# A gated recurrence with a top-80 expert layer: full-width last loads, quarter-sized zero writes, unchained scatters and a shorter ranking

## The chip, the cores and the metric

One NeuronCore of a Trainium2 chip runs the whole program. The metric is the device time of one execution in microseconds (us); the runs shown are three executions of the kernel before. Matrix work runs on TensorE (PE; PEld are its weight loads), elementwise work on VectorE (DVE), ScalarE (ACT) and GpSimd (POOL), and transfers are issued by SyncE's queue (SP), a few by POOL and ACT. All transfers run on the same 16 DMA engines.

## The reference

The first half is a gated recurrence over 4 sequences of 5056 steps and 256 channels; the second half sends each of the 20224 results to one of 8 experts, keeps the 80 best per expert, and leaves every other row of the output zero.

```python
f = lower_bound + (1 - lower_bound) * sigmoid(f_logit)
for t in range(S):                       # S = 5056
    h = f[:, t] * h + (1 - f[:, t]) * x[:, t]
    y[:, t] = h
X = y.reshape(20224, 256)
logits = X @ w_gate                      # 8 experts
expert = argmax(logits); gate = softmax(logits)[expert]
out = zeros(20224, 256)
for e in range(8):
    tok = the 80 tokens of expert e with the largest gate
    out[tok] = gate[tok] * (relu(X[tok] @ w1[e]) @ w2[e])   # F = 1024
```

## The kernel before

**The stream.** Time is cut into 10 groups of 512 steps (the last has 448), and each group into 4 units, one for each sequence: 40 units. A unit `n` has one 512 KB load of `f_logit` and one of `x` (`load_f`, `load_x`, L235 and L241), issued three units ahead by SP; the last group loads 448 KB on 112 partitions. ACT makes the gate (`gate`, L249), POOL multiplies (`enter`, L253), PE transposes both into channels-by-time in PSUM (`to_channels`, L261, tiles `sp` and `up`), ACT turns `sp` into the decay in SBUF (`decay`, L271), and DVE runs the recurrence as two scans per unit (`scan`, L278). PE then makes the unit's gate logits (`logits`, L292). Once per group ACT copies the logits aside (`aside`), PE turns them by token (`by_token`, tile `lt`, L306), and DVE finds maxima and choices (`maxima` L318 and L319, `choice` L328 and L332). The PSUM pool of `up` has three buffers, two per unit; the turned candidates have a bank of their own (`ct`).

**The zeros.** The 20.7 MB of zeros of the output are written by SP from a zeroed DRAM tile, in 160 pieces of 128 KB (eighths of 20 strips, `clear_some`, L156): two behind each unit's loads for units 4 to 31, 16 behind the last load, 8 behind each of the first three weight keys, 16 more, and 4 behind each of the next 12 keys (`BESIDE`).

**The ranking.** When the last scan is done, POOL sums the exponentials of old groups (`halved`, L352) and makes their worths (`worth`, L366), PE turns them (`candidates`), DVE takes the top 8 of each of 8 parts (`peaks`, L383), `best` ranks those 64 into 12 (L386 to L389), which are put ahead of the two newest groups in `fresh`, and a second `best` ranks that. Selection, slots and token numbers follow up to L605.

**The experts.** Weights come in 16 keys of two 512 KB halves, through a ring of 6 halves (`weights`, L500 for w1 and L504 for w2), so key i waits until key i-3 has been used. The order is (1,0) (2,0) (1,1) (1,2) (2,1) (1,3) (2,2) (1,4) (2,3) (1,5) (2,4) (1,6) (2,5) (1,7) (2,6) (2,7), where (1,e) is w1 of expert e and (2,e) its w2. Expert e's 80 tokens are copied out of SBUF by DVE, ACT and POOL together (`gather`, L655, 24, 32 and 24 copies), scaled by DVE (L662), multiplied by w1 (`hidden`, L673) and w2 (`result`, L688), and scaled again (`finish`, L694); POOL sends them to their rows by one indirect DMA per expert (`scatter`, L697). A scatter may be sent only when all zeros have been issued, and waits for them to land. Each engine works its instructions in the order in which this loop writes them:

```python
for e in range(1, E):
    if e + 2 < E: gather(e + 2)
    if e + 1 < E:
        ps = hidden(e + 1); relu(e + 1, ps); more(1)   # one more key, and its zeros
    y_ps = result(e); more(1)
    if e + 2 < E: scaled(e + 2)
    finish(e, y_ps)
    scatters(e - 1)            # sends all that wait, if no zeros are left
```

Three keys are loaded before this loop's part of the code and three `more(1)` stand ahead of the loop.

Of the kernel before, what the change touches and what calls it, by code (L numbers as in the profile page):

```python
# [17 lines left out]
P = 128  # L18
TOP = 8
AWAY = 1.0e6  # L20
PAD = 104
# [6 lines left out]
def kernel(  # L28
# [25 lines left out]
    BESIDE = 4  # L54
# [5 lines left out]
    def first(g):  # L60
        return g * G
# [11 lines left out]
    assert B == R and C == R * R and all(size(g) % C == 0 for g in range(n_grp))  # L73
# [47 lines left out]
    NEW = DEEP + (n_grp - OLD) * P  # L121
# [3 lines left out]
    tops = consts.tile([P, NP, TOP], F32, name="tops")  # L125
    prev = consts.tile([P, 2 * TOP], F32, name="prev")
# [21 lines left out]
    ZQ = 8  # L148
# [4 lines left out]
    def clear(k, q=None):  # L153
        n = min(ZR, N // P - k) * D
        rows = slice(0, P) if q is None else ds(q * QP, QP)
# [28 lines left out]
    psu = psum.enter_context(tc.tile_pool(name="psu", bufs=3, space=PSUM))  # L184
    plg = psum.enter_context(tc.tile_pool(name="plg", bufs=1, space=PSUM))

    with tc.tile_pool(name="ld", bufs=4) as ld, \
# [47 lines left out]
        def load_f(n):  # L235
            g, b = divmod(n, B)
            fs[n] = ld.tile([P, R, D], F32, name="f_t", tag="f_t")
            nc.sync.dma_start(
                out=fs[n][:run(g)], in_=tiles(f_logit, b, g))

        def load_x(n):  # L241
            g, b = divmod(n, B)
            xs[n] = ld.tile([P, R, D], F32, name="x_t", tag="x_t")
            nc.sync.dma_start(
                out=xs[n][:run(g)], in_=tiles(x, b, g))

        def gate(n):
            s_t = sts[n] = fs.pop(n)[:run(n // B)]
            nc.scalar.activation(s_t, s_t, ACT.Sigmoid, scale=-1.0)  # L249

        def enter(n):
            u_t = uts[n] = xs.pop(n)[:run(n // B)]
            (nc.gpsimd if n else nc.vector).tensor_tensor(u_t, sts[n], u_t, ALU.mult)  # L253

        def to_channels(n, src, dst, pool, tag, in_time):
            k = run(n // B)
            for o in range(DC):
                ps = pool.tile([P, G], F32, name=tag, tag=tag)
                for r in range(R):
                    at = ps[:, r:R * k:R] if in_time else ps[:, ds(r * k, k)]  # L260
                    nc.tensor.transpose(at, src[n][:, r, ds(o * P, P)], ident[:k, :k])  # L261
                dst[n, o] = ps[:, :R * k]
            del src[n]
# [5 lines left out]
        def decay(n):  # L269
            for o in range(DC):  # L270
                nc.scalar.activation(columns(n, o).rearrange("c (p r) -> c p r", r=R),  # L271
                                     sps.pop((n, o)).rearrange("c (r p) -> c p r", r=R),
                                     ACT.Identity, scale=nomlb[:, ds(o, 1)], bias=1.0)

        def scan(n):
            for o in range(DC):
                h = columns(n, o)
                nc.vector.tensor_tensor_scan(  # L278
                    h, h, ups.pop((n, o)),
                    h_all[:, o, ds(spot(n) - 1, 1)] if n >= B else 0.0, ALU.mult, ALU.add)  # L280
# [60 lines left out]
        def sums(g0, g1):  # L341
            n = g1 - g0
            sms[g0] = gsm.tile([P, 1, C], F32, name="sm", tag="sm%d" % g0)
            nc.vector.tensor_reduce(
                sms[g0], exs.pop(g0).rearrange("p (g c e) -> p g c e", c=C, e=E), AX.X, ALU.add)
# [29 lines left out]
        def candidates(g0):  # L375
            ct = plg.tile([P, 2 * P], F32, name="ct", tag="ct")
            turned(g0, 2, ct)
            nc.scalar.copy(cand[:, ds(g0 * P, 2 * P)], ct)

        def peaks(g):  # L380
            for i, (g0, lo) in enumerate(parts):
                if g0 == g:
                    nc.vector.max(out=tops[:, i], in_=cand[:, lo:(g + 2) * P:2])  # L383

        def best(vals, src, rest):
            nc.vector.max(out=vals[:, :TOP], in_=src)  # L386
            nc.vector.match_replace(out=rest, in_to_replace=vals[:, :TOP], in_values=src,
                                    imm_value=GONE)
            nc.vector.max(out=vals[:, TOP:], in_=rest)  # L389
# [16 lines left out]
        done_f = []  # L406

        for n in range(-AHEAD, n_unit):
            m = n + AHEAD
            for k in (m, m + 1):  # L410
                if k < n_unit and k not in done_f and (k == m or m >= LAST - 2):
                    done_f.append(k)
                    load_f(k)
            unit(load_x, m)
            if n == -1:
                spread_zeros()
            if n == -AHEAD:
                setup()
            if n + 2 < LAST:
                unit(gate, n + 2)  # L420
            unit(enter, n + 2)
            if n + 1 < LAST:
                unit(lambda m: to_channels(m, sts, sps, pss, "sp", False), n + 1)
                unit(decay, n + 1)
            if n + 2 == LAST - 1:
                gate(LAST)
            if n + 2 == LAST:
                to_channels(LAST, sts, sps, pss, "sp", False)
                decay(LAST)
                aside(OLD)  # L430
                exponentials(0, OLD)
            unit(lambda m: to_channels(m, uts, ups, psu, "up", True), n + 1)
# [14 lines left out]
        for k in range(0, OLD, OLD // 2):  # L447
            halved(k, OLD // 2)
            for g in range(k, k + OLD // 2, 2):
                worth(g, k, 2, nc.gpsimd)  # L450
                candidates(g)
                if g == 0:
                    aside(n_grp - 1)
                elif g == 2:
                    by_token(n_grp - 1)
        g = n_grp - 1
        peaks(0)
        peaks(2)
        maxima(g)
        fresh = plg.tile([P, NEW], F32, name="fresh", tag="lg")  # L460
        busy(pss, 8, "sp")
        exponentials(g, g + 1, aside=True)
        choice(g, nc.vector)
        sums(OLD, OLD + 1)
        worth(OLD, OLD, 1, nc.gpsimd)
        turned(OLD, 1, fresh[:, ds(DEEP, P)])
        sums(g, g + 1)
        worth(g, g, 1, nc.vector)
        turned(g, 1, fresh[:, ds(DEEP + P, P)])
# [24 lines left out]
    def weights(which, e):  # L494
        halves = []
        for i in range(2):
            t = wring.tile([P, DC * FH], F32, name="w_sb", tag="w_sb")
            if which == 1:
                t = t.rearrange("p (o f) -> p o f", o=DC)
                nc.sync.dma_start(out=t, in_=w1[e][:, ds(i * FH, FH)].rearrange(  # L500
                    "(o p) f -> p o f", p=P))
            else:
                t = t.rearrange("p (c d) -> p c d", c=CH)
                nc.sync.dma_start(out=t, in_=w2[e][ds(i * FH, FH)].rearrange(  # L504
                    "(c p) d -> p c d", p=P))
            halves.append(t)
        return halves
# [27 lines left out]
    with tc.tile_pool(name="sel", bufs=1) as sel:  # L535
        vals2 = consts.tile([P, 2 * TOP], F32, name="vals2")
        rest = sel.tile([P, NEW], F32, name="rest")
        best(vals2, fresh, rest)
# [70 lines left out]
    def settle():  # L609
# [12 lines left out]
        nc.vector.tensor_reduce(d[:, 5:6], tops[:, :, TOP - 1], AX.X, ALU.max)  # L622
# [14 lines left out]
    def experts(again):  # L637
        with tc.tile_pool(name="xp", bufs=2) as xp, \
# [68 lines left out]
            waiting = []  # L707
# [135 lines left out]
```

## Time and profile before

| what | value |
|---|---|
| three executions | 260.38, 262.93, 266.25 us (median 262.93) |
| the profiled execution | 260.38 us, span 258.6 us, 1.8 us around it |
| PE, DVE, ACT, POOL busy | 75%, 62%, 53%, 53% of the span |
| DMA | 81.13 MB, mean 314 GB/s over the span |
| largest shares of the chain that ended last | DMA 37%, PE 23%, DVE 12% |

The span runs from the first to the last instruction. A busy share is an average over stages with different limits: stream (to about 142 us), ranking (to about 165 us), experts (to about 235 us) and a tail of scatters. The profile's page cuts the span into 40 slices of 6.5 us and gives the DMA share of each.

### The profile page before, as it was taken

The page shows a single profiled execution, that of the slowest core. Times are in us where ns is not written, and L with a number is a line of the kernel's source. Part 1 is how long each engine was busy: PE and PEld are TensorE (multiplying, and loading weights), DVE is VectorE, ACT ScalarE, POOL GpSimd, SP SyncE. Part 2 cuts the span into 40 slices and gives each one's busy share as a digit, 9 for nine tenths or more (in the row PEclk, how much of TensorE's full clock was granted, in tenths as well). Part 3 has the DMA queues.
Part 4 walks back from the last instruction along what each step waited for, and adds up shares of the span by engine and source line. Part 5 has one row for each costly group of instructions (what it writes and reads, how often), then busy time and mean ns, then how long its engine had stood idle before and what let it go on. Part 6 is the DMA issues. An engine that isn't in the chain of part 4 may idle for free.

```text
span 258.6 us, 6254 instructions
## 1 busy us (share of the span) xinstructions
PE 193.7 (75%) x1841; PEld 159.1 (62%) x1841; DVE 160.7 (62%) x430; ACT 136.6 (53%) x430; POOL 136.4 (53%) x279
## 2 busy tenths in 40 slices
PE   1879989898889898988486758979999888882000
PEld 1757777676767676766364558868888657651000
DVE  4566988989898989897638488457555335000000
ACT  3657877676778787866744315465666551100000
POOL 2457878777777777776473710457444400012221
PEclk9997999999999999999979579999999999999555
DMA  6999999999999999999965888769999999961010
GB/s 190 402 418 416 421 415 426 414 416 417 420 414 415 418 414 420 414 370 274 297 212 161 286 273 297 205 202 340 324 351 371 345 354 362 326 249 35 20 31 15
DMA packets 30811, 81.13 MB, mean 314 GB/s; under 512 B 5040, under 2 KB 13360, under 8 KB 28336
## 3 DMA queue, kind: packets, MB, share of 16 engines
q1 hardware_dynamic: 29840, 79.97, 84.1%
q0 software_dynamic: 384, 0.66, 0.9%
q8 instruction: 17, 0.28, 0.4%
q14 instruction: 26, 0.21, 0.2%
q10 hardware_dynamic: 544, 0.01, 0.1%
HBM read 78.91 MB, written 22.41 MB: 392 GB/s over the span
## 4 chain that ended last, share of the span: by engine, by line
DMA 37%; PE 23%; DVE 12%; issue 8%; ACT 8%; SPq 6%; POOL 3%; ACTq 1%; POOLq 0%; DVEq 0%
DMA w_sb<-in_moe_w_dram 11%; DMA f_t<-in_f_logit_dram 10%; DMA x_t<-in_x_dram 8%; DVE h_all L278 6%; PE up L261 5%; PE h_ps L673 5%; PE sp L261 5%; DMA out_dram<-y,goal 5%; SPq L156 5%; PE lg L292 3%; ACT h_all L271 3%; PE y_ps L688 3%; DMA wg<-in_moe_w_gate_dram 2%; DVE eq L328 2%; ACT xe L655 2%
## 5 line engine op out<-in xcount | busy, mean ns | idle before, releaser
L253 POOL TENSOR_TENSOR x_t<-f_t,x_t 128x1024 f32<-128x1024 f32 (+1 forms) x39 | 92.3, 2369 | 32.6 <-DMA x_t<-in_x_dram 22.6
L278 DVE TENSOR_TENSOR_SCAN h_all<-h_all,up 128x512 f32<-128x512 f32 (+1 forms) x80 | 94.8, 1242 | 9.3 <-PE up L261 6.0
L249 ACT ACTIVATE f_t<-f_t 128x1024 f32<-128x1024 f32 (+1 forms) x40 | 42.4, 1059 | 31.9 <-DMA f_t<-in_f_logit_dram 31.9
L261 PE MATMUL up<-ident,x_t 128*128 128x128 f32 (+1 forms) x320 | 47.0, 287 | 13.6 <-DVE h_all L278 7.6
L271 ACT ACTIVATE h_all<-sp,nomlb 128x512 f32<-128x512 f32 (+1 forms) x80 | 49.9, 673 | 6.5 <-PE sp L261 6.3
L261 PE MATMUL sp<-ident,f_t 128*128 128x128 f32 (+1 forms) x320 | 46.0, 289 | 7.3 <-ACT f_t L249 5.8
L261 PEld LDWEIGHTS up<-ident,x_t 128*128 128x128 f32 (+1 forms) x320 | 37.2, 147 | 18.9 <-DVE h_all L278 8.4
L261 PEld LDWEIGHTS sp<-ident,f_t 128*128 128x128 f32 (+1 forms) x320 | 36.4, 147 | 15.8 <-issue 13.0
L655 POOL COPY xe<-h_all 128x2 f32 x192 | 23.9, 187 | 22.6 <-DVE xt L662 8.8
L655 ACT COPY xe<-h_all 128x2 f32 x256 | 25.4, 190 | 14.1 <-issue 10.6
L688 PE MATMUL y_ps<-w_sb,hid 128*80 128x256 f32 x128 | 29.3, 381 | 4.4 <-DMA w_sb<-in_moe_w_dram 2.9
L673 PE MATMUL h_ps<-xt,w_sb 128*128 128x80 f32 x256 | 30.0, 276 | 3.5 <-DMA w_sb<-in_moe_w_dram 1.8
L673 PEld LDWEIGHTS h_ps<-xt,w_sb 128*128 128x128 f32 x256 | 29.2, 192 | 5.1 <-PE y_ps L688 1.9
L292 PE MATMUL lg<-h_all,wg 128*32 128x128 f32 (+1 forms) x640 | 27.3, 288 | 6.1 <-ACT ls L300 4.5
L655 DVE COPY xe<-h_all 128x2 f32 x192 | 22.6, 172 | 12.5 <-issue 12.5
L697 POOL DMA_INDIRECT out_dram<-y,goal x8 | 7.5, 938 | 42.5 <-DMA w_sb<-in_moe_w_dram 25.8
L688 PEld LDWEIGHTS y_ps<-w_sb,hid 128*80 128x80 f32 x128 | 18.5, 150 | 13.0 <-ACT hid L681 4.8
L292 PEld LDWEIGHTS lg<-h_all,wg 128*32 128x32 f32 x640 | 15.8, 110 | 13.4 <-ACT ls L300 6.4
L694 DVE TENSOR_SCALAR y<-y_ps,gsl 80x256 f32<-80x256 f32 x8 | 3.8, 479 | 24.0 <-PE y_ps L688 24.0
L681 ACT ACTIVATE hid<-h_ps 128x320 f32<-128x320 f32 x16 | 6.6, 431 | 17.4 <-PE h_ps L673 17.4
L166 PEld LDWEIGHTS warm<-ident 128*128 128x128 f32 x92 | 12.5, 220 | 0.1
L166 PE MATMUL warm<-ident 128*128 128x128 f32 x92 | 12.5, 302 | 0.0
(125 smaller groups left out, 101.1 us busy)
## 6 DMA issues: line engine op xcount, KB each, us to landing
out_dram<-z_dram SPq DMA_DIRECT2D x152, 128.0 KB, 5.8
f_t<-in_f_logit_dram SPq DMA_DIRECT2D x36, 512.0 KB, 6.2
x_t<-in_x_dram SPq DMA_DIRECT2D x36, 512.0 KB, 6.2
w_sb<-in_moe_w_dram SPq DMA_DIRECT2D x32, 512.0 KB, 5.7
f_t<-in_f_logit_dram SPq DMA_DIRECT2D x4, 448.0 KB, 8.4
x_t<-in_x_dram SPq DMA_DIRECT2D x4, 448.0 KB, 9.7
z_dram<-zero SPq DMA_DIRECT2D x1, 1024.0 KB, 9.1
out_dram<-z_dram SPq DMA_DIRECT2D x8, 96.0 KB, 5.4
```

What stands on the lines that cost most here:

```text
L156: nc.sync.dma_start(out=out_z[rows, ds(k * D, n)], in_=z_dram[rows, :n])
L166: nc.tensor.matmul(warm, ident, ident, start=True, stop=True)
L249: nc.scalar.activation(s_t, s_t, ACT.Sigmoid, scale=-1.0)
L253: (nc.gpsimd if n else nc.vector).tensor_tensor(u_t, sts[n], u_t, ALU.mult)
L261: nc.tensor.transpose(at, src[n][:, r, ds(o * P, P)], ident[:k, :k])
L271: nc.scalar.activation(columns(n, o).rearrange("c (p r) -> c p r", r=R), sps.pop((n, o)).rearrange("c (r p) -> c p r", r=R), ACT.Identity, ...
L278: nc.vector.tensor_tensor_scan(h, h, ups.pop((n, o)), h_all[:, o, ds(spot(n) - 1, 1)] if n >= B else 0.0, ALU.mult, ALU.add)
L292: nc.tensor.matmul(lgs[g][ds(r * LC, LC), b, :k], wg[:, o], h[:, r], start=o == 0, stop=o == DC - 1, skip_group_check=True)
L655: copy(X[e][:, :, ds(k + j, 1)], h_all[:, :, ds(v, 1)])
L673: nc.tensor.matmul(h_ps[:, c], halves[i][:, o, ds(c * P, P)], xt[:, o], start=o == 0, stop=o == DC - 1, skip_group_check=True)
L688: nc.tensor.matmul(y_ps, hid[:, c], halves[c // CH][:, c % CH], start=c == 0, stop=c == FC - 1)
L697: nc.gpsimd.indirect_dma_start(out=out, out_offset=bass.IndirectOffsetOnAxis(ap=goal[:, ds(e, 1)], axis=0), in_=Y.pop(e), in_offset=None, ...
```

## The change

- The last group's loads take 512 steps, beginning 64 steps early, so that they fill 128 partitions; `decay` and `scan` skip the 64 (`lead`). The special order of the last `f` loads and gates goes.
- Zeros are written in quarters (256 KB, `ZQ = 4`), several of a strip in one DMA: one quarter behind every second unit from 5 to 31, six behind the last load, five behind each half of the first three keys, three behind each later key while there are any.
- The `up` pool has four PSUM buffers; the candidates' tile shares the `sp` pool's two.
- In the ranking, the sums of groups 4 to 7 go from POOL to one DVE reduction, one pair's worths go to DVE, group 8's sums go to POOL; the top 8 lists are written straight into `fresh` (320 columns in place of 268), the ranking of 64 into 12 goes, and so do 8 warming matmuls.
- The scatters no longer wait for one another.

```diff
+    def lead(g):
+        return G - size(g)
     def tiles(ap, b, g):
-        return ap[b, ds(first(g), size(g))].rearrange("(p r) d -> p r d", r=R)
+        return ap[b, ds(first(g) - lead(g), G)].rearrange("(p r) d -> p r d", r=R)
...
-    ZQ = 8
+    ZQ = 4
...
     def clear_some(m):
-        for k, q in zeros[:m]:
-            clear(k, q)
-        del zeros[:m]
+        while m > 0 and zeros:
+            k, q = zeros[0]
+            n = min(m, ZQ - q)
+            clear(k, q, n)
+            del zeros[:n]
+            m -= n
...
-    psu = psum.enter_context(tc.tile_pool(name="psu", bufs=3, space=PSUM))
+    psu = psum.enter_context(tc.tile_pool(name="psu", bufs=4, space=PSUM))
...
             if n + AHEAD == LAST:
-                clear_some(2 * ZQ)
-            elif B <= n < n_unit - 2 * B:
-                clear_some(2)
+                clear_some(6)
+            elif B <= n < n_unit - 2 * B and n % 2:
+                clear_some(1)
...
-        for k in range(0, OLD, OLD // 2):
-            halved(k, OLD // 2)
-            for g in range(k, k + OLD // 2, 2):
-                worth(g, k, 2, nc.gpsimd)
-                candidates(g)
...
+        HALF = OLD // 2
+        halved(0, HALF)
+        sums(HALF, OLD)
+        worth(0, 0, 2, nc.gpsimd)
+        candidates(0)
+        worth(OLD - 2, HALF, 2, nc.vector)
+        aside(g)
+        worth(2, 0, 2, nc.gpsimd)
+        candidates(2)
+        by_token(g)
+        candidates(OLD - 2)
+        worth(HALF, HALF, 2, nc.gpsimd)
+        candidates(HALF)
...
-        peaks(4)
-        peaks(6)
-        rest = gsm.tile([P, NP * TOP], F32, name="rest", tag="eq")
-        best(prev, tops.rearrange("p n t -> p (n t)"), rest)
-        nc.vector.tensor_copy(fresh[:, :DEEP], prev[:, :DEEP])
-        nc.scalar.copy(cand[:, OLD * P:], fresh[:, DEEP:])
+        for k in (2, OLD - 2, HALF):
+            peaks(k, fresh)
+        nc.scalar.copy(cand[:, OLD * P:], fresh[:, NP * TOP:])
+        eighths = fresh[:, TOP - 1:NP * TOP:TOP]
+        last_of = consts.tile([P, NP], F32, name="last_of")
+        nc.scalar.copy(last_of, eighths)
...
     for key in order[:3]:
-        w_sb[key] = weights(*key)
-        clear_some(ZQ)
-    clear_some(len(zeros) - BESIDE * (E - 2) * 2)
+        w_sb[key] = weights(*key, 5)
...
             def scatter(e):
-                nc.gpsimd.indirect_dma_start(
+                one = nc.gpsimd.indirect_dma_start(
...
+                for other in sent:
+                    tc.declare_no_dep(one.ins, other.ins,
+                                      reason="a token is in one expert's list only")
+                sent.append(one)
             def more(m):
                 for key in late[:m]:
                     w[key] = weights(*key)
-                    clear_some(BESIDE)
+                    clear_some(3)
```

## Rows read from the trace of the kernel before

**Rows 1.** The page: the span, and the GB/s of its 40 slices.
```profile
span 258.6 us, 6254 instructions
...
GB/s 190 402 418 416 421 415 426 414 416 417 420 414 415 418 414 420 414 370 274 297 212 161 286 273 297 205 202 340 324 351 371 345 354 362 326 249 35 20 31 15
```

**Rows 2.** Stages: engines' busy us, PE clock, DMA share, GB/s.
```profile
40.00:110.00 70.00, 61.73 (x744) 50.75 (x740) 63.77 (x68) 53.62 (x75) 54.36 (x29) 1.00 1.02 417
...
120.00:125.00 5.00, 4.84 (x63) 3.96 (x64) 3.35 (x7) 3.51 (x7) 2.38 (x1) 1.00 1.03 272
...
130.00:135.00 5.00, 4.66 (x43) 3.62 (x43) 2.19 (x2) 2.11 (x4) 4.04 (x2) 0.75 0.59 192
...
180.00:229.90 49.90, 44.62 (x302) 36.76 (x301) 20.39 (x147) 21.29 (x174) 13.07 (x106) 1.00 1.00 350
```

**Rows 3.** Timeline of DVE in the stream: start, us, instruction, idle before it.
```profile
33.38 0.29 DVE L318 TENSOR_REDUCE mx<-lt 128x16 f32<-128x128 f32 x1 [1.50 <-PE lt L306]
...
95.63 0.29 DVE L318 TENSOR_REDUCE mx<-lt 128x16 f32<-128x128 f32 x1 [0.95 <-PE lt L306]
...
108.10 0.29 DVE L318 TENSOR_REDUCE mx<-lt 128x16 f32<-128x128 f32 x1 [0.95 <-PE lt L306]
```

**Rows 4.** Timeline of DVE in the last two groups.
```profile
121.58 0.29 DVE L318 TENSOR_REDUCE mx<-lt 128x16 f32<-128x128 f32 x1 [1.70 <-PE lt L306]
...
130.10 2.19 DVE L278 TENSOR_TENSOR_SCAN h_all<-h_all,up 128x448 f32<-128x448 f32 x2 [2.95 <-PE up L261]
136.53 0.29 DVE L318 TENSOR_REDUCE mx<-lt 128x16 f32<-128x128 f32 x1 [4.24 <-PE lt L306]
...
139.66 2.18 DVE L278 TENSOR_TENSOR_SCAN h_all<-h_all,up 128x448 f32<-128x448 f32 x2
```

**Rows 5.** DMA issues by line: count, KB each, median us to landing.
```profile
x_t<-in_x_dram SPq DMA_DIRECT2D x36, 512.0 KB, 6.2
...
x_t<-in_x_dram SPq DMA_DIRECT2D x4, 448.0 KB, 9.7
```

**Rows 6.** Timeline of the ranking's end, 149 to 152 us.
```profile
149.94 0.23 DVE L386 MAX8 prev<-tops 128x8 f32<-128x64 f32 x1
...
150.85 0.17 DVE L474 COPY fresh<-prev 128x12 f32<-128x12 f32 x1
...
151.52 0.45 DVE L386 MAX8 vals<-fresh 128x8 f32<-128x268 f32 x1 [0.49 <-ACT cand L475]
```

**Rows 7.** Timeline of SP's queue.
```profile
138.98 0.92 SPq L500 DMA_DIRECT2D w_sb<-in_moe_w_dram  x2
...
171.99 1.04 SPq L500 DMA_DIRECT2D w_sb<-in_moe_w_dram  x2
```

**Rows 8.** Timeline of POOL among the experts and in the tail.
```profile
178.18 3.05 POOL L655 COPY xe<-h_all 128x2 f32 x24 [1.42 <-DVE xe L655]
...
229.93 1.12 POOL L697 DMA_INDIRECT out_dram<-y,goal  x1 [25.80 <-DMA w_sb<-in_moe_w_dram]
...
250.18 0.91 POOL L697 DMA_INDIRECT out_dram<-y,goal  x1 [2.17 <-DMA out_dram<-y,goal]
253.26 0.91 POOL L697 DMA_INDIRECT out_dram<-y,goal  x1 [2.17 <-DMA out_dram<-y,goal]
```

**Rows 9.** Timeline of PE and, between, of DVE.
```profile
129.03 1.71 PE L261 MATMUL up<-ident,x_t 112*128 112x112 f32 x8 [3.33 <-POOL x_t L253]
...
134.37 0.93 PE L261 MATMUL up<-ident,x_t 112*128 112x112 f32 x8
...
168.66 3.80 PE L673 MATMUL h_ps<-xt,w_sb 128*128 128x80 f32 x32 [1.11 <-DVE xt L662]
...
226.96 7.43 PE L688 MATMUL y_ps<-w_sb,hid 128*80 128x256 f32 x32 [1.29 <-DMA w_sb<-in_moe_w_dram]
...
234.44 0.48 DVE L694 TENSOR_SCALAR y<-y_ps,gsl 80x256 f32<-80x256 f32 x1 [3.30 <-PE y_ps L688]
```

**Rows 10.** The w2 loads by line: all halves' times to landing.
```profile
DMA to landing us min/median/max: 4.8/6.0/7.3
```

More of the change, by code (lines that the diff above doesn't have):

```diff
@@ L20 @@
 AWAY = 1.0e6
-PAD = 104
+PAD = 48
 NONE = -64.0
@@ L53 @@
     BY_DVE = 4
-    BESIDE = 4
     assert N % P == 0 and D % P == 0 and F % P == 0 and C * E == P
@@ L67, in run @@
         return size(g) // R
+    def lead(g):
+        return G - size(g)
     def tiles(ap, b, g):
-        return ap[b, ds(first(g), size(g))].rearrange("(p r) d -> p r d", r=R)
+        return ap[b, ds(first(g) - lead(g), G)].rearrange("(p r) d -> p r d", r=R)
     W = P // R
-    assert B == R and C == R * R and all(size(g) % C == 0 for g in range(n_grp))
+    assert B == R and C == R * R and all(size(g) % C == 0 for g in range(n_grp)) and S >= G
     consts = ctx.enter_context(tc.tile_pool(name="consts", bufs=1))
@@ L147, with clear @@
     clears = range(0, N // P, ZR)
-    ZQ = 8
+    ZQ = 4
     QP = P // ZQ
     zeros = [(k, q) for k in clears for q in range(ZQ)]
-    def clear(k, q=None):
+    def clear(k, q=0, m=ZQ):
         n = min(ZR, N // P - k) * D
-        rows = slice(0, P) if q is None else ds(q * QP, QP)
+        rows = ds(q * QP, m * QP)
         nc.sync.dma_start(out=out_z[rows, ds(k * D, n)], in_=z_dram[rows, :n])
     def clear_some(m):
-        for k, q in zeros[:m]:
-            clear(k, q)
-        del zeros[:m]
+        while m > 0 and zeros:
[4 more added lines that the diff above has]
+            m -= n
     def busy(pool, m, tag):
@@ L233, in spread_zeros, with load @@
                               in_=zero.unsqueeze(1).broadcast_to([P, m, ZC]))
-        def load_f(n):
+        def load(n):
             g, b = divmod(n, B)
             fs[n] = ld.tile([P, R, D], F32, name="f_t", tag="f_t")
[L238 to L242, printed above, removed]
+            nc.sync.dma_start(out=fs[n], in_=tiles(f_logit, b, g))
             xs[n] = ld.tile([P, R, D], F32, name="x_t", tag="x_t")
-            nc.sync.dma_start(
-                out=xs[n][:run(g)], in_=tiles(x, b, g))
+            nc.sync.dma_start(out=xs[n], in_=tiles(x, b, g))
         def gate(n):
-            s_t = sts[n] = fs.pop(n)[:run(n // B)]
+            s_t = sts[n] = fs.pop(n)
             nc.scalar.activation(s_t, s_t, ACT.Sigmoid, scale=-1.0)
         def enter(n):
-            u_t = uts[n] = xs.pop(n)[:run(n // B)]
+            u_t = uts[n] = xs.pop(n)
             (nc.gpsimd if n else nc.vector).tensor_tensor(u_t, sts[n], u_t, ALU.mult)
         def to_channels(n, src, dst, pool, tag, in_time):
-            k = run(n // B)
             for o in range(DC):
-                ps = pool.tile([P, G], F32, name=tag, tag=tag)
+                ps = dst[n, o] = pool.tile([P, G], F32, name=tag, tag=tag)
                 for r in range(R):
-                    at = ps[:, r:R * k:R] if in_time else ps[:, ds(r * k, k)]
-                    nc.tensor.transpose(at, src[n][:, r, ds(o * P, P)], ident[:k, :k])
-                dst[n, o] = ps[:, :R * k]
+                    at = ps[:, r::R] if in_time else ps[:, ds(r * P, P)]
+                    nc.tensor.transpose(at, src[n][:, r, ds(o * P, P)], ident)
             del src[n]
@@ L342, in sums @@
             n = g1 - g0
-            sms[g0] = gsm.tile([P, 1, C], F32, name="sm", tag="sm%d" % g0)
+            sms[g0] = gsm.tile([P, n, C], F32, name="sm", tag="sm%d" % n)
+            ex = exs.pop(g0) if n == 1 else cand[:, ds(g0 * P, n * P)]
             nc.vector.tensor_reduce(
-                sms[g0], exs.pop(g0).rearrange("p (g c e) -> p g c e", c=C, e=E), AX.X, ALU.add)
+                sms[g0], ex.rearrange("p (g c e) -> p g c e", c=C, e=E), AX.X, ALU.add)
         def halved(g0, n):
@@ L375, in candidates, with peaks @@
         def candidates(g0):
-            ct = plg.tile([P, 2 * P], F32, name="ct", tag="ct")
+            ct = pss.tile([P, G], F32, name="ct", tag="sp")[:, :2 * P]
             turned(g0, 2, ct)
             nc.scalar.copy(cand[:, ds(g0 * P, 2 * P)], ct)
-        def peaks(g):
+        def peaks(g, tops):
             for i, (g0, lo) in enumerate(parts):
                 if g0 == g:
[L383 to L389, printed above, removed]
+                    nc.vector.max(out=tops[:, ds(i * TOP, TOP)], in_=cand[:, lo:(g + 2) * P:2])
         def unit(f, m):
@@ L405 @@
         LAST = n_unit - 1
-        done_f = []
         for n in range(-AHEAD, n_unit):
[L409 to L414, printed above, removed]
+            unit(load, n + AHEAD)
             if n == -1:
@@ L418 @@
                 setup()
-            if n + 2 < LAST:
-                unit(gate, n + 2)
+            unit(gate, n + 2)
             unit(enter, n + 2)
[L422 to L429, printed above, removed]
+            unit(lambda m: to_channels(m, sts, sps, pss, "sp", False), n + 1)
+            unit(lambda m: to_channels(m, uts, ups, psu, "up", True), n + 1)
+            unit(decay, n + 1)
+            if n == LAST - 2:
                 aside(OLD)
+            elif n == LAST - 1:
                 exponentials(0, OLD)
-            unit(lambda m: to_channels(m, uts, ups, psu, "up", True), n + 1)
             unit(scan, n)
@@ L492, with weights @@
         order += ([(1, e + 1)] if e + 1 < E else []) + [(2, e)]
-    def weights(which, e):
+    def weights(which, e, beside=0):
         halves = []
@@ L506, in weights @@
             halves.append(t)
+            clear_some(beside)
         return halves
@@ L537 @@
         rest = sel.tile([P, NEW], F32, name="rest")
-        best(vals2, fresh, rest)
+        nc.vector.max(out=vals2[:, :TOP], in_=fresh)
+        nc.vector.match_replace(out=rest, in_to_replace=vals2[:, :TOP], in_values=fresh,
+                                imm_value=GONE)
+        nc.vector.max(out=vals2[:, TOP:], in_=rest)
         vals = vals2[:, :DEEP]
@@ L703, in more @@
                     w[key] = weights(*key)
-                    clear_some(BESIDE)
+                    clear_some(3)
                 del late[:m]
-            waiting = []
+            waiting, sent = [], []
             def scatters(e):
```

28 lines of the change are left out of this document (11 added, 17 removed).

## The prediction

> **What bounds the kernel now.** I read the page first, for its span and its slices [rows 1], then the table of stages [rows 2], then the timelines of DVE, SP, POOL and PE around the edits. The reader should see four stages with four limits. In the stream (up to the last scan, which ends at 139.66 + 2.18 = 141.84) the DMA engines are full at 417 GB/s while DVE is busy 63.77 of 70 us: two limits that lie close together [rows 2]. One group takes 12.45 us, (108.10 - 33.38) / 6, and in it DVE stands still for about one us, ahead of the maxima [rows 3]. In the last two groups the rate falls to 272 GB/s with the DMA engines still full [rows 2]: the 448 KB loads land in 9.7 us, the 512 KB ones in 6.2 [rows 5], and DVE waits 1.70, 2.95 and 4.24 us [rows 4]. Ranking and slots follow as a chain up to the first expert's matmul at 168.66 [rows 9]. Then the DMA engines are full again at 350 GB/s [rows 2], with weights and zeros in one SP queue. At 229.93 the last zeros are in, and eight scatters follow one by one, 3.08 us apart, up to 253.26 and the end at 258.6 [rows 1, 8].
>
> **The stream.** Units 4 to 31 get one 256 KB quarter per two units instead of two 128 KB eighths per unit. A group then moves 4.19 MB of loads and 0.52 MB of zeros (before 1.05 MB), which takes 4.72 / 0.417 = 11.3 us. DVE's own work is 63.77 / 70 x 12.45 = 11.35 us, so the group can't get under about 11.4. The fourth `up` buffer lets PE turn a whole unit while the one ahead is still scanned. I take 11.8, nearer to the floor than to 12.45, because two limits that close never fill each other. Over six groups that is 3.9 us; the ends are 0 and 6.0.
>
> **The last two groups.** From 108.10 to 141.84 are 33.7 us, of which DVE waits 1.70 + 2.95 + 4.24 = 8.9 [rows 3, 4]. Loads on 128 partitions carry 64 KB more each, but their row is 6.2 us against 9.7 [rows 5], and no zeros stand among them. The full-width transposes and scans cost nothing: scans still run over 448 steps, and PE has waits to spare here. I keep 0.5 us ahead of each of two maxima and take 7.9; the ends are 2.95 (only the wait behind the slow transfer goes) and 8.9. The last scan then ends at 130.0.
>
> **The ranking.** Ranking 64 into 12 is gone, 149.94 to 151.02, 1.08 us [rows 6]. Three passes over 320 columns instead of 268 cost 0.45 x 52 / 268 = 0.09 each, and the second ACT copy, which DVE waits for as it does now [rows 6], about 0.2. POOL is relieved, but between the last scan and the maxima of the newest group stands the same chain. I take 0.7; the ends are 0 and 1.5. The removed warming matmuls ran while DVE worked. The first expert's matmul comes at 168.66 - 3.9 - 7.9 - 0.7 = 156.2.
>
> **The zeros that moved.** Counted out: 14 + 6 quarters in the stream, 30 behind the first three keys, 30 behind the next ten. The first weight issue, now 138.98 [rows 7], needs the stream's buffers and moves to 127.2. From there 30 quarters and 6 halves, 7.86 + 3.15 = 11.0 MB, take 31.5 us at 350 GB/s, up to 158.7. Key 3 can't be issued before the first expert's matmul has freed its buffers, now 171.99 - 168.66 = 3.3 us behind its start [rows 7, 9], so at 159.5. The extra zeros there are just hidden, by the ranking; without that cover each quarter costs 0.75 us. Behind the experts it is not hidden: ten keys of 1.05 + 0.79 MB take 18.35 / 0.350 = 52.4 us. The same sum on the kernel before (19.92 MB from 171.99) gives 228.9, where the first scatter was let go at 229.93, so I add 1.0: the last zeros land at 159.5 + 53.4 = 212.9.
>
> **The scatters, and what they stand ahead of.** Zeros now run out with key 12, (2,5), which is issued in turn e = 4 of the loop. Before they ran out with key 14, in turn e = 5. So the waiting scatters 0 to 3 are put into POOL's queue ahead of `gather(7)`, which before stood ahead of all scatters. They wait for the zeros; behind them wait POOL's 24 copies of expert 7, for these DVE's scaling, and for that `hidden(7)`, `result(6)` and `result(7)` on PE. The working: four scatters that no longer wait for each other, 0.91 us of POOL each plus 0.1 (bounds 0.91, and 3.08 as now); register loads 1.42 and copies 3.05 [rows 8]; scaling and start 0.8. `hidden(7)` begins at 212.9 + 4.0 + 4.5 + 0.8 = 222.2. It takes 3.8 us and two results 7.43 [rows 9]. PE will have stood idle for some 8 us, and after an idle 3.33 us eight transposes took 1.71 us, where later 0.93 were enough [rows 9], at a granted clock of 0.75 over those 5 us [rows 2]; I add 1.5 for such a start (bounds 0.8 and 3). The Trainium skill (TensorE: Matmul & The Clock Gate, HAM oscillation) tells of waits on data after which the array begins again at half of its 2.4 GHz; the trace agrees, in that 0.75 over 5 us is part 1.2 and part 2.4 GHz. By that page with all of `hidden(7)` at half rate, 3.8 us would be added instead of 1.5 and the time below would be 246. PE ends at 234.9; the last scaling ends 0.5 later [rows 9], the last scatter begins at 235.5, and from there to the end are 258.6 - 253.26 = 5.3 us [rows 1, 8]. The span is 240.8; with the 1.8 us around the profiled execution, 242.6. That execution was the fastest of three and 2.5 us under their median, so I add half of that: **244**.
>
> **Rivals.**
> First, the scatters don't hold up `gather(7)`, because the zeros land earlier than counted or POOL gets to its copies first. Then the last three keys land 3.15 / 0.350 = 9.0 us behind the zeros, PE ends 4.5 later as now (229.93 to 234.39), and the time is 235. Against it stands the order of the loop, in which nothing lets POOL pass the scatters. 16%.
> Second, the stream keeps its 12.45 us, because the wait for the maxima comes from the order on PE and not from DMA: 3.9 us come back, 248; with the last groups gaining only 2.95 as well, 253. For it speaks that DVE is already 91% busy. 14%.
> Third, the scatters stay chained by something else than the declared order, such as a shared semaphore: 4 x (3.08 - 1.0) = 8.3 us ahead of `gather(7)`, 252. No row excludes it. 9%.
> Fourth, on the other side: the scatters ahead of `gather(7)` are now sent while weights stream, and each is held as long as a transfer of that stage, up to 7.3 us [rows 10]. Four of 0.91 + 7.3 cost 28.8 us more, 273. It decides from 7.1 us a scatter, where the time passes 268. The Trainium skill (DMA: Bandwidth & Descriptors, Queues, rings and completion order) says that each DMA engine takes turns between its queue rows packet by packet, by which a scatter would not stand behind the weights; no scatter of this trace ran beside them. Against this rival: only 9 us of weights are left by then, which can hold two scatters, not four. 4%.
>
> **How the numbers follow.** My forecast has 52% (its own range 238 to 250), the rivals as given, 5% are for the unforeseen. The bounds of the terms reach down to about 239 and up to 253; with the first rival below, the range 233 to 253 leaves out the fourth and parts of the others. A measurement of this kernel can tell about 2% from no change, 257.7 to 268.2 around the median of 262.93. Forecast and three rivals lie under it: faster 0.92, same 0.04, slower 0.04.
>
> **What would show it.** In the profile after: a group of 11.4 to 12.0 us between two maxima, and no DVE wait over 1 us in the last two groups; the last scan ending at 127 to 133; the first expert's matmul at 153 to 160; DMA full from the first weights on, with no rate under 330 GB/s among the experts; POOL's first scatters near 213 and ahead of its last 24 copies, about 1 us apart; a PE gap of 7 to 9 us ahead of `hidden(7)`; about 5 us from the last scatter to the end. I am wrong if the group stays over 12.3, if the scatters stand 3 us apart, or if PE has no such gap.

## The result, and the profile after

The changed kernel takes 240.98 us, the median of four executions (239.59 to 242.16), against 264.0 us for the kernel before (260.38 to 266.25). The ratio is 0.921 with a 95% interval of 0.909 to 0.932. The prediction was 244 with a range of 233 to 253. The profiled execution took 241.05 us, with a span of 239.2.

The page of the changed kernel: the span, the rate in 40 slices of 6.0 us, and one row of the DMA issues (count, KB each, median us from issue to landing). They answer [rows 1] and [rows 5].

```profile
span 239.2 us, 6094 instructions
GB/s 166 399 416 422 416 415 420 417 418 418 418 417 419 414 421 418 417 423 411 408 66 395 356 402 371 272 159 331 324 404 404 406 403 410 400 355 73 1 18 22
x_t<-in_x_dram SPq DMA_DIRECT2D x40, 512.0 KB, 7.1
```

All forty `x` loads now have one shape, and there are two dips in the DMA: one at the end of the stream (66 GB/s) and one near 157 us (159 GB/s).

The table of stages of the changed kernel answers [rows 2]. Columns: the stretch, its length, then busy us and instructions of PE, PEld, DVE, ACT and POOL, PE's granted clock, the DMA share and GB/s.

```profile
40.00:110.00 70.00, 66.32 (x819) 55.26 (x818) 67.41 (x75) 58.70 (x81) 61.12 (x31) 1.00 1.03 418
120.00:125.00 5.00, 4.37 (x73) 3.65 (x71) 4.62 (x8) 2.90 (x5) 2.09 (x2) 1.00 0.14 32
140.00:145.00 5.00, 5.00 (x26) 5.00 (x26) 4.63 (x22) 4.08 (x16) 0.35 (x1) 0.54 1.04 397
155.00:160.00 5.00, 3.77 (x32) 3.62 (x32) 3.07 (x26) 3.49 (x34) 3.05 (x24) 1.00 0.37 124
180.00:190.00 10.00, 8.40 (x55) 6.65 (x54) 3.78 (x28) 4.19 (x35) 3.02 (x24) 1.00 1.05 404
218.19:225.28 7.09, 7.09 (x33) 7.09 (x34) 0.46 (x2) 0.44 (x1) 1.61 (x2) 0.50 0.08 23
```

The stream still runs at full DMA, but DVE is now busy 67.41 of 70 us instead of 63.77. Among the experts the same full DMA moves 404 GB/s instead of 350. PE is at or near the lower of its two clock levels, 1.2 of 2.4 GHz, in two places: in the ranking from 130 to 145 (0.50 up to 140, then 0.54), and from 218.19 to 225.28, which is `hidden(7)` (0.50).

DVE's timeline of the changed kernel answers [rows 3, 4] (start, us, engine, line, operation, tiles, count, and in brackets the idle time before it and what ended it).

```profile
33.00 0.29 DVE L316 TENSOR_REDUCE mx<-lt 128x16 f32<-128x128 f32 x1 [1.35 <-PE lt L304]
100.91 0.29 DVE L316 TENSOR_REDUCE mx<-lt 128x16 f32<-128x128 f32 x1 [0.17 <-PE lt L304]
103.81 0.74 DVE L326 SCALAR_TENSOR_TENSOR eq<-cand,revexp 128x128 f32<-128x128 f32 x1
124.15 2.18 DVE L276 TENSOR_TENSOR_SCAN h_all<-h_all,up 128x448 f32<-128x448 f32 x2
131.15 0.29 DVE L316 TENSOR_REDUCE mx<-lt 128x16 f32<-128x128 f32 x1 [0.70 <-PE lt L304]
146.29 0.16 DVE L578 COPY off<-sums_p 128x1 f32<-128x1 f32 x1 [1.03 <-PE sums_p L572]
```

A group takes (100.91 - 33.00) / 6 = 11.32 us where it took 12.45, and the wait ahead of the maxima is down from about 1 us to 0.17. The last scan ends at 126.33 instead of 141.84, and the waits of 1.70, 2.95 and 4.24 us are gone.

The experts and the tail, on POOL and PE, answer [rows 8, 9].

```profile
210.06 1.13 POOL L684 DMA_INDIRECT out_dram<-y,goal  x1 [26.73 <-DMA w_sb<-in_moe_w_dram]
211.49 0.92 POOL L684 DMA_INDIRECT out_dram<-y,goal  x1 [0.30 <-issue]
213.94 0.92 POOL L684 DMA_INDIRECT out_dram<-y,goal  x1 [0.30 <-issue]
214.86 2.94 POOL L642 COPY xe<-h_all 128x2 f32 x24
233.66 0.92 POOL L684 DMA_INDIRECT out_dram<-y,goal  x1 [2.54 <-DVE y L681]
```

```profile
154.98 3.80 PE L660 MATMUL h_ps<-xt,w_sb 128*128 128x80 f32 x32 [1.12 <-DVE xt L649]
218.19 7.09 PE L660 MATMUL h_ps<-xt,w_sb 128*128 128x80 f32 x32 [8.14 <-DVE xt L649]
225.08 7.79 PE L675 MATMUL y_ps<-w_sb,hid 128*80 128x256 f32 x32
```

The scatters follow one another in 1.22 to 1.43 us instead of 3.08. But four of them, and the wait for the zeros (26.73 us of idle POOL), stand ahead of the last 24 copies, so PE stands still for 8.14 us and then needs 7.09 us for what took 3.80 at 154.98.

### The profile page after: what moved, and what is told of

It reads as the page before. It is cut to its first block, busy times and chain, and to the rows that moved or that the text cites. A ratio compares the mean times of both kernels' runs of the same rounds, so it can differ in the third digit from the quotient of the medians.

```text
span 239.2 us, 6094 instructions
## 1 busy us (share of the span) xinstructions
PE 192.1 (80%) x1825; PEld 161.0 (67%) x1825; DVE 158.3 (66%) x427; ACT 136.7 (57%) x431; POOL 135.4 (57%) x277
## 4 chain that ended last, share of the span: by engine, by line
DMA 40%; PE 29%; ACT 12%; POOL 7%; issue 4%; DVE 2%; SPq 2%; ACTq 1%; POOLq 1%; DVEq 0%
DMA f_t<-in_f_logit_dram 20%; DMA w_sb<-in_moe_w_dram 10%; PE h_ps L660 8%; DMA x_t<-in_x_dram 7%; PE y_ps L675 6%; PE sp L259 4%; ACT h_all L268 4%; ACT f_t L248 3%; POOL x_t L252 3%; DMA wg<-in_moe_w_gate_dram 3%; PE lg L290 3%; PE warm L170 2%; ACT xe L642 2%; SPq L156 2%; PE up L259 2%
## 5 line engine op out<-in xcount | busy, mean ns | idle before, releaser
L252 POOL TENSOR_TENSOR x_t<-f_t,x_t 128x1024 f32<-128x1024 f32 x39 | 92.5, 2378 | 19.6 <-DMA x_t<-in_x_dram 17.8
L268 ACT ACTIVATE h_all<-sp,nomlb 128x512 f32<-128x512 f32 (+1 forms) x80 | 50.1, 676 | 11.0 <-PE sp L259 10.9
L248 ACT ACTIVATE f_t<-f_t 128x1024 f32<-128x1024 f32 x40 | 42.5, 1063 | 15.0 <-DMA f_t<-in_f_logit_dram 14.8
L259 PE MATMUL sp<-ident,f_t 128*128 128x128 f32 x320 | 45.7, 287 | 6.5 <-ACT f_t L248 6.0
L259 PE MATMUL up<-ident,x_t 128*128 128x128 f32 x320 | 43.9, 282 | 5.2 <-POOL x_t L252 3.5
L259 PEld LDWEIGHTS sp<-ident,f_t 128*128 128x128 f32 x320 | 36.1, 145 | 14.4 <-issue 13.2
L660 PE MATMUL h_ps<-xt,w_sb 128*128 128x80 f32 x256 | 33.3, 294 | 11.8 <-DVE xt L649 9.3
L259 PEld LDWEIGHTS up<-ident,x_t 128*128 128x128 f32 x320 | 37.1, 145 | 8.2 <-POOL x_t L252 6.0
L660 PEld LDWEIGHTS h_ps<-xt,w_sb 128*128 128x128 f32 x256 | 32.4, 209 | 13.6 <-issue 8.8
L642 ACT COPY xe<-h_all 128x2 f32 x256 | 25.4, 190 | 14.1 <-issue 12.3
L290 PEld LDWEIGHTS lg<-h_all,wg 128*32 128x32 f32 x640 | 15.4, 108 | 11.3 <-ACT ls L298 4.6
L649 DVE TENSOR_SCALAR xt<-xe,omlb 128x80 f32<-128x80 f32 x16 | 3.5, 258 | 15.2 <-POOL xe L642 11.7
L170 PEld LDWEIGHTS warm<-ident 128*128 128x128 f32 x76 | 10.9, 230 | 0.1
```

The source lines that it names most:

```text
L170: nc.tensor.matmul(warm, ident, ident, start=True, stop=True)
L259: nc.tensor.transpose(at, src[n][:, r, ds(o * P, P)], ident)
L290: nc.tensor.matmul(lgs[g][ds(r * LC, LC), b, :k], wg[:, o], h[:, r], start=o == 0, stop=o == DC - 1, skip_group_check=True)
L642: copy(X[e][:, :, ds(k + j, 1)], h_all[:, :, ds(v, 1)])
L660: nc.tensor.matmul(h_ps[:, c], halves[i][:, o, ds(c * P, P)], xt[:, o], start=o == 0, stop=o == DC - 1, skip_group_check=True)
```

## The experiments

Each experiment edits the changed kernel, except the one that edits the kernel before. Those with one profiled execution alone have one time; two were timed in more executions and have an interval. A difference of 2 or 3 us between single times is not far from the spread of one kernel (239.59 to 242.16), so the small effects are read from the traces.

**The place of the scatters in POOL's queue.** The early scatters are held back from the end of turn 4 to the end of turn 5, so `gather(7)`, which stands at the start of turn 5, goes ahead of them.

```diff
-                if not zeros:
+                if not zeros and e >= E - 4:
```

> The changed kernel with one edit: the waiting scatters are sent one turn later, behind POOL's copies for expert 7. Theory (the scatters' place in POOL's queue costs the time): hidden(7) starts right behind result(5), near 210 us, at the full clock; PE ends near 221 instead of 232.9, the last scatter starts near 222 and the time is 229 to 230. Rival (the end is set by the last weights, and the gap on PE is only their wait): the gap of 8 us stays ahead of hidden(7) or comes back ahead of result(6) or result(7), and the time stays at 240 to 242.

Measured: 228.71 us (227.83 to 228.88), 12.3 us under the changed kernel's median; against the kernel before in the same session the ratio is 0.872 (0.865 to 0.879). PE's and POOL's timelines of this kernel:

```profile
210.06 3.77 PE L660 MATMUL h_ps<-xt,w_sb 128*128 128x80 f32 x32 [0.69 <-DMA w_sb<-in_moe_w_dram]
213.67 7.07 PE L675 MATMUL y_ps<-w_sb,hid 128*80 128x256 f32 x32
209.66 1.12 POOL L684 DMA_INDIRECT out_dram<-y,goal  x1 [18.85 <-DMA w_sb<-in_moe_w_dram]
```

`hidden(7)` starts at 210.06 and now waits for its weights alone; it takes 3.77 us, the results 7.07, and the last scatter comes at 221.53 instead of 233.66. The scatters themselves begin at the same time (209.66 and 210.06). So the 12 us are the price of their place in the queue: 8.1 us later, and 3.3 + 0.7 us slower because PE had stood still.

**The scatters chained again.** The declaration that they are independent is taken out; all else stays.

```diff
-                for other in sent:
-                    tc.declare_no_dep(one.ins, other.ins,
-                                      reason="a token is in one expert's list only")
-                sent.append(one)
```

> The changed kernel with the scatters waiting for one another as before. Theory: each of scatters 0 to 3 takes 3.1 to 3.6 us of POOL instead of 1.25, expert 7's copies come 7 to 9 us later and with them the end: 248 to 250 us. Rival (only the last scatter counts, and by then the queue is empty): 241 us.

Measured: 249.26 us. POOL and PE of this kernel:

```profile
208.59 1.12 POOL L684 DMA_INDIRECT out_dram<-y,goal  x1 [26.06 <-DMA w_sb<-in_moe_w_dram]
214.59 0.92 POOL L684 DMA_INDIRECT out_dram<-y,goal  x1 [4.87 <-DMA out_dram<-y,goal]
217.67 0.92 POOL L684 DMA_INDIRECT out_dram<-y,goal  x1 [2.17 <-DMA out_dram<-y,goal]
222.36 2.95 POOL L642 COPY xe<-h_all 128x2 f32 x24 [0.68 <-issue]
225.71 7.09 PE L660 MATMUL h_ps<-xt,w_sb 128*128 128x80 f32 x32 [17.00 <-DVE xt L649]
```

The chain of waits for landings is what the declaration removes: 8.3 us here. The condition of the third rival is not met in the changed kernel. Its price of 8.3 us agrees in the total and not in its parts: from the first scatter to the copies 13.8 us pass instead of 4.8, because the first scatter, sent while weights stream, holds the second up for 6.0 us and the next follow in 3.08; against that the zeros landed 1.5 us earlier in this run.

**The declaration alone, in the kernel before.**

```diff
-                nc.gpsimd.indirect_dma_start(
+                one = nc.gpsimd.indirect_dma_start(
...
+                for other in sent:
+                    tc.declare_no_dep(one.ins, other.ins,
+                                      reason="a token is in one expert's list only")
+                sent.append(one)
```

> The kernel before with one edit, the scatters no longer wait for one another. Theory: eight scatters 1.25 us apart from 229.9 on, the last starts near 238.7, the span ends near 244 and the time is 246 (against 260 to 266). Rival (something else keeps them in order, such as a shared semaphore): 3.1 us apart, 260 or more.

Measured: 248.12 us, where the kernel before took 263.15 in the same session.

```profile
233.13 1.12 POOL L697 DMA_INDIRECT out_dram<-y,goal  x1 [28.20 <-DMA w_sb<-in_moe_w_dram]
241.89 0.92 POOL L697 DMA_INDIRECT out_dram<-y,goal  x1 [0.30 <-issue]
```

Eight scatters take 8.8 us from first to last, where they took 23.3 (229.93 to 253.26). This one part is worth 15 us where the scatters end the program. In the changed kernel the stretch from the first scatter to the end is 239.2 - 210.06 = 29.1 us, no shorter than before (258.6 - 229.93 = 28.7): what the declaration gives there, the place in the queue takes back, and the gain that is left is that the zeros land 19.9 us earlier.

**Zeros in eighths again, the same bytes.** Every DMA of zeros carries 128 KB, as in the kernel before; the counts are doubled, so the same zeros are written in the same places, but no two go in one DMA.

```diff
-    ZQ = 4
+    ZQ = 8
...
-            n = min(m, ZQ - q)
+            n = 1
...
-                clear_some(6)
+                clear_some(12)
...
-                clear_some(1)
+                clear_some(2)
...
-        w_sb[key] = weights(*key, 5)
+        w_sb[key] = weights(*key, 10)
...
-                    clear_some(3)
+                    clear_some(6)
```

> The changed kernel with the same bytes of zeros at the same places, but in pieces of 128 KB as before, one DMA each. Theory (the higher rate among the experts, 404 GB/s against 350 before, comes from larger transfers): 350 GB/s between 180 and 200 us, the last zeros land 4 to 6 us later and the time is 245 to 247. Rival (the rate comes from the mix of zeros and weights, or from the stage beginning earlier): 400 GB/s and 241 us.

Measured: 259.92 us. A stage of this kernel, the same stretch of the kernel with the scatters held back (403 GB/s) below it, and two rows of SP's queue:

```profile
180.00:210.00 30.00, 23.17 (x139) 17.95 (x138) 9.40 (x68) 11.66 (x101) 3.00 (x24) 0.93 0.95 313
```

```profile
180.00:210.00 30.00, 24.55 (x157) 19.10 (x154) 11.94 (x84) 12.19 (x102) 6.30 (x49) 1.00 1.05 403
```

```profile
123.76 6.40 SPq L156 DMA_DIRECT2D out_dram<-z_dram  x10
166.71 1.37 SPq L485 DMA_DIRECT2D w_sb<-in_moe_w_dram  x2
```

The expectation had the direction and not the size: the same bytes take 19 us more. SP needs 0.64 us for each piece (6.40 / 10), and at 0.95 of the DMA share 313 GB/s are moved where the larger pieces move 403 at 1.05. So a piece costs both SP's time and more DMA time per byte. The two show in different places. Key 3 is issued at 166.71, 9.7 us later than in the changed kernel (157.02), although the first expert's matmul even begins 0.85 us earlier (154.13): up to there SP is issuing pieces without a pause, and the DMA share is 0.85 over 125 to 140 us. From key 3 to the first scatter (228.75) 62.0 us pass instead of 53.0. That is the 19 us in two halves; in the second half SP's time and the slower transfers were not told apart.

**The stream's zeros doubled.** Fourteen quarters are written a second time in the stream, so that it carries as many bytes as before; all other edits stay.

```diff
+    later = zeros[40:54]
...
+            elif B <= n < n_unit - 2 * B:
+                clear(*later.pop(), 1)
```

> The changed kernel with the stream's zeros doubled again, one quarter behind every unit from 4 to 31 as many bytes as before; the 14 extra quarters are written twice, so later stages are unchanged. Theory A (the stream was bound by transfers): a group takes 12.3 to 12.5 us again instead of 11.3, the last scan ends 6 to 7 us later and the time is 247 to 248. Theory B (the fourth PSUM buffer shortened the group): 11.3 to 11.5 us and 241.

Measured: 249.07 us. DVE's timeline:

```profile
33.44 0.29 DVE L317 TENSOR_REDUCE mx<-lt 128x16 f32<-128x128 f32 x1 [1.45 <-PE lt L305]
107.96 0.29 DVE L317 TENSOR_REDUCE mx<-lt 128x16 f32<-128x128 f32 x1 [0.84 <-PE lt L305]
110.86 1.36 DVE L327 SCALAR_TENSOR_TENSOR eq<-cand,revexp 128x128 f32<-128x128 f32 x1
```

A group takes (107.96 - 33.44) / 6 = 12.42 us, against 12.45 before, and the time is a little over the 247 to 248 that were expected. With the bytes put back the four buffers alone bring 0.03 us a group, so the gain of the stream hangs on the bytes; the second rival, that the order on PE holds the maxima up, is refuted.

**Three `up` buffers instead of four.**

```diff
-    psu = psum.enter_context(tc.tile_pool(name="psu", bufs=4, space=PSUM))
+    psu = psum.enter_context(tc.tile_pool(name="psu", bufs=3, space=PSUM))
```

> The changed kernel with three PSUM buffers for the unit's product instead of four. Theory A (transfers bound the stream): a group stays at 11.3 to 11.5 us and the time at 241. Theory B (the fourth buffer did it): 12.3 us a group, 247.

Measured: 243.71 us.

```profile
34.31 0.29 DVE L316 TENSOR_REDUCE mx<-lt 128x16 f32<-128x128 f32 x1 [1.50 <-PE lt L304]
103.21 0.29 DVE L316 TENSOR_REDUCE mx<-lt 128x16 f32<-128x128 f32 x1 [0.96 <-PE lt L304]
106.11 0.27 DVE L326 SCALAR_TENSOR_TENSOR eq<-cand,revexp 128x128 f32<-128x128 f32 x1
```

The wait of about one us comes back (0.96), yet a group is only 0.16 longer, (103.21 - 34.31) / 6 = 11.48: what DVE waits here it saves in `eq`, 0.27 instead of 0.74. The wait ahead of the maxima is there with few buffers (0.96) and, with four, under more bytes too (0.84 above), but how long a group takes follows the bytes. The buffer's worth by these two profiles is 2.6 us at the last scan, of which 1.3 are already there at the first maxima; with one time of this kernel the size is uncertain.

**The last loads on 112 partitions again.** `tiles`, `load`, `gate`, `enter`, `to_channels`, `decay` and `scan` go back to the form of before for the last group; no zeros stand among these loads, as in the changed kernel.

```diff
-        return ap[b, ds(first(g) - lead(g), G)].rearrange("(p r) d -> p r d", r=R)
+        return ap[b, ds(first(g), size(g))].rearrange("(p r) d -> p r d", r=R)
...
-            nc.sync.dma_start(out=xs[n], in_=tiles(x, b, g))
+            nc.sync.dma_start(out=xs[n][:run(g)], in_=tiles(x, b, g))
```

> The changed kernel with the last group's loads on 112 partitions as before, without the 64 steps in front. Theory (the narrow loads are slow in themselves): they land in 9 us or more, DVE waits 4 to 8 us in the last group, the last scan ends at 130 to 134 instead of 126.2 and the time is 245 to 249. Rival (the old order of the last loads and the zeros among them made the waits): DVE waits under 1 us and 241.

Measured: 244.55 us. Its DMA issues with the rate while these loads run, and DVE:

```profile
x_t<-in_x_dram SPq DMA_DIRECT2D x4, 448.0 KB, 10.0
105.00:110.00 5.00, 3.86 (x54) 2.89 (x52) 5.00 (x5) 3.32 (x6) 3.39 (x3) 1.00 1.05 259
```

```profile
125.61 0.29 DVE L318 TENSOR_REDUCE mx<-lt 128x16 f32<-128x128 f32 x1 [2.71 <-PE lt L306]
128.74 2.17 DVE L278 TENSOR_TENSOR_SCAN h_all<-h_all,up 128x448 f32<-128x448 f32 x2
```

With fewer bytes each, these loads take 9.2 (`f_logit`) and 10.0 us (`x`) to land. With the DMA engines full they move 259 GB/s, where the slices of the changed kernel between 108 and 120 us show 408 to 423. DVE's waits in the last group sum to 4.7 us, the longest 2.71, and the last scan ends at 130.91 instead of 126.33. The 128 partitions are worth 4.6 of the 8.3 us that the last groups gained. The other 3.7 are left for what differs besides (the order of the last loads and transposes, the buffers, what zeros run beside them); they were not separated. Zeros among the last group's loads are not part of it: in the kernel before SP issues none between 108.6 and 122.4 us either.

**A version that beats both.** The scatters held back, 12 quarters instead of 6 behind the last load, and 12 warming matmuls behind the last transposes.

```diff
-                clear_some(6)
+                clear_some(12)
...
+        busy(pss, 12, "sp")
...
-                if not zeros:
+                if not zeros and e >= E - 4:
```

> The changed kernel with three edits: the scatters sent one turn later, twelve instead of six quarters behind the last load, and twelve warming matmuls on PE behind the last turned group. Theory (the transfers stand still for 5 us between 120 and 125 us, and PE's half clock at 140 us delays the slots): the first expert's matmul comes 1 to 2 us earlier than 155.0 and the zeros end two keys earlier, so PE ends near 217 and the time is 224 to 226. Rival (the experts' stage is bound by PE and the ring, not by transfers): 228 to 229, as with the late scatters alone.

Measured: 225.77 us (224.46 to 226.89), against the kernel before a ratio of 0.854 (0.846 to 0.863). The stage at the end of the stream and two rows of PE:

```profile
120.00:125.00 5.00, 4.20 (x72) 3.48 (x69) 4.62 (x8) 2.98 (x4) 1.93 (x2) 1.00 0.87 302
139.52 3.73 PE L170 MATMUL warm<-ident 128*128 128x128 f32 x32
153.63 3.80 PE L661 MATMUL h_ps<-xt,w_sb 128*128 128x80 f32 x32 [1.09 <-DVE xt L650]
```

The DMA's dip is filled (share 0.87 instead of 0.14), 32 warming matmuls take 3.73 us (5.75 in the changed kernel, shown below), and the first expert's matmul comes 1.35 us earlier. What each of the three edits is worth in the total was not measured.

## Why the prediction was right, and which of its steps were not

The sum ended 1.6 us above the measured span (240.8 against 239.2), and the place where gain is given back was named: the queue ahead of `gather(7)`. Behind the sum stand errors of up to 8 us that cancel, so that it came this near is partly luck. Three of the signs it named did not come: the group (11.32) and the last scan (126.33) lie under their ranges, and the rate among the experts falls below 330 GB/s.

**The stream: right mechanism, mis-sized.** 3.9 us were counted, 6.8 came (six groups of 11.32 instead of 12.45). "A group can't get under about 11.4" took DVE's 11.35 us of work as fixed. But DVE's own work fell to 67.41 / 70 x 11.32 = 10.9 us, and that is `eq`: 1.22 to 1.35 us in the kernel before (40 to 110 us), 0.74 at 103.81 here, 1.36 with the bytes put back, 0.27 with three buffers. Two rows of POOL, of the kernel with the doubled zeros and of the one with three buffers, show why:

```profile
109.70 2.38 POOL L253 TENSOR_TENSOR x_t<-f_t,x_t 128x1024 f32<-128x1024 f32 x1 [0.69 <-PE sp L260]
```

```profile
103.71 2.37 POOL L252 TENSOR_TENSOR x_t<-f_t,x_t 128x1024 f32<-128x1024 f32 x1 [0.23 <-ACT f_t L248]
```

In the first, POOL multiplies until 112.08 and `eq`, begun at 110.86, ends at 112.22; in the second POOL is done at 106.08, before `eq` begins at 106.11, and it takes 0.27. Where they overlap, `eq` ends 0.14 us behind POOL's instruction. The Trainium skill (SBUF — State Buffer, Who interferes with whom) says that a DVE instruction with two inputs from SBUF shares its second read with POOL's reads, and that the one that comes later waits; the trace agrees. So the limit that was left is DMA: 11.3 us by bytes, 11.32 measured. The argument "two limits that close never fill each other" failed here.

**The last groups: right.** 7.9 us were counted, 8.3 came (33.7 to 25.4), and no wait over 1 us is left. The 128 partitions are 4.6 of them, and what the other 3.7 are stays open.

**The ranking: wrong sign.** A gain of 0.7 us was counted; it lost 1.8: from the last scan's end to the first expert's matmul 126.33 to 154.98 are 28.65 us, before 26.8. Two rows of DVE in the changed kernel and POOL's first sums, then two rows of DVE and one of PE in the kernel before:

```profile
134.12 1.99 DVE L382 MAX8 fresh<-cand 128x8 f32<-128x128 f32 x6 [0.57 <-PE fresh L371]
136.69 0.50 DVE L522 MAX8 vals<-fresh 128x8 f32<-128x320 f32 x1 [0.58 <-ACT last_of L460]
125.75 1.64 POOL L351 TENSOR_TENSOR cand<-cand 128x256 f32<-128x256 f32 x3 [1.03 <-ACT cand L337]
```

```profile
145.33 0.29 DVE L318 TENSOR_REDUCE mx<-lt 128x16 f32<-128x128 f32 x1
149.05 0.86 DVE L383 MAX8 tops<-cand 128x8 f32<-128x128 f32 x4
155.05 4.40 PE L166 MATMUL warm<-ident 128*128 128x128 f32 x32
```

Between the newest maxima and `vals` 5.54 us pass instead of 6.19, the 0.65 that were counted, but the direct lists did not bring them: from the last lists to `vals` it is 2.57 us (134.12 to 136.69) instead of 2.47 (149.05 to 151.52), because six lists of 0.33 us stand there instead of four of 0.22 and the ranking of 64 (why one list takes longer was not tested). The gain lies ahead of the lists, where DVE no longer waits 1.03 us for ACT's newest exponentials. And two things were missed. First, "between the last scan and the maxima stands the same chain": it does not begin at the scan any more. ACT's table load and exponentials now end at 125.69, and POOL's sums begin at 125.75, only 0.58 us ahead of the scan's end; before they began at 140.18, 1.66 ahead of it. The maxima of the newest group (131.15 above) come 4.82 us behind the scan instead of 3.49 (145.33): 1.3 us. Second, "the removed warming matmuls ran while DVE worked" priced them by the time that they took and not by the clock that they kept. PE's timeline of the changed kernel:

```profile
140.38 5.75 PE L170 MATMUL warm<-ident 128*128 128x128 f32 x32
```

With the clock at 0.54 over 140 to 145, mostly the lower level, the 32 that stayed take 5.75 us instead of 4.40, and DVE waits 1.03 us for `sums_p` behind them; from `vals` to the first expert's matmul 18.3 us pass instead of 17.1, which is 1.2. In the kernel before the clock was 0.54 over 145 to 150, where the eight ran, and 0.86 over 155 to 160. No run puts the eight alone back, so that they were the cause is argued. The last experiment, with 12 put ahead in another place, runs the 32 in 3.73 us, and from the scan to the matmul it takes 27.5: that gives back 1.2 us. So 1.3 + 1.2 were lost and 0.65 won.

**The zeros and the weights: errors that cancel.** The last zeros were counted 53.4 us behind key 3, and 53.0 were measured (157.02 to 210.06):

```profile
157.02:210.06 53.04, 46.08 (x309) 37.82 (x308) 26.11 (x198) 27.09 (x233) 16.71 (x134) 1.00 0.99 369
```

The rate of 350 GB/s was taken over from the kernel before, that is, from pieces of 128 KB; larger pieces go at 404, and 18.35 MB would take 45.4 us. The experiment with eighths shows that the rate hangs on the pieces. That was the step that failed: the change was costed by its bytes, and a quarter in place of two eighths at nothing. Then "DMA full from the first weights on" failed too: the share is 0.37 at 155 to 160, because the faster zeros are done before the first expert's matmul frees the ring's buffers, for which SP waits up to 11.4 us. The rate is 124 GB/s there and 333 and 279 in the ten us after. Of the 7.6 us that the larger pieces won, some 4.6 go with this dip (369 GB/s over the whole stretch instead of 404). The other 3.0 go with bytes that were not counted: 53.04 us at 369 GB/s are 19.6 MB, 1.2 more than 18.35, and what stands behind the zeros in SP's queue are the weights of the last three keys.

**The scatters and the queue: right, and the most that the prediction foresaw.** Scatters 1.22 to 1.43 us apart (1.0 counted), four of them ahead of the last 24 copies, a gap of 8.14 us on PE (some 8 counted), 5.5 us from the last scatter to the end (5.3). The 1.42 us that were counted for register loads did not come: the copies start at 214.86, where the fourth scatter ends, so `hidden(7)` starts 8.13 us behind the zeros instead of 9.3. The row that they were read from puts this idle time down to a wait for DVE, not to register loads [rows 8]. The start at low clock was mis-sized: 1.5 us added with bounds of 0.8 and 3, 3.3 measured at a granted clock of 0.50 throughout, with 7.79 instead of 7.07 for the results too. The row that the 1.5 came from, eight transposes in 1.71 us at 129.03, ran at 0.53 itself; the 0.75 that was read beside it is the mean of 130 to 135. The prediction's other estimate, all of `hidden(7)` at half rate, put this term at 3.8 and was nearer. The Trainium skill (TensorE: Matmul & The Clock Gate, HAM oscillation) has PE begin at half rate after such a wait; the trace agrees (0.50).

**The rivals.** The first (no delay of `gather(7)`) was made to happen by the first experiment: counted 235, measured 228.7 with the scatters held back; the 6 us between were not followed up. The second is refuted by the doubled zeros. The third does not hold, and its price of 8.3 us is what the chain costs, by parts that differ from the counted ones. Its 3.08 us a scatter were read from the last rows of [rows 8]; the first three gaps of the kernel before are 3.55, 3.41 and 4.05 us. The fourth holds for one scatter: 6.0 us beside the weights, but the next took 3.08, and in the changed kernel none was waited for.

## What to carry to other kernels

A DMA that waits in an engine's queue holds all compute behind it: when such a wait is moved earlier in the order, look at what stands behind it, for here the same scatters, put behind one gather, were worth 12 us. Cost a transfer by its number of pieces as well as its bytes, and take a rate only from transfers of the same size. When filler work is removed or a stage gets shorter, ask what it kept running, such as PE's clock or the DMA engines.

## What the runs showed of the hardware

- 128 KB pieces from DRAM to DRAM cost 0.64 us of SP's queue each (10 in 6.40 us), and a stage of weights with six of them to a key reached 313 GB/s; with merged ones of the same bytes 403. In the stream of the kernel before, where a fifth of the bytes were such pieces, 417 were reached all the same.
- A 448 KB load on 112 partitions lands in 9.2 to 10.0 us, a 512 KB load on 128 in 7.1; with the DMA engines full the former move 259 GB/s, the latter over 400.
- The same DVE instruction (`eq`) takes 0.27 to 1.36 us, as POOL's multiplication overlaps it or not.
- After 8.14 us without work PE needed 7.09 us, at a granted clock of 0.50, for matmuls that take 3.77 to 3.80 otherwise.
